# Attention emitted as products and sums, a new order of the first loads, and float64 weights converted in five instructions

## The chip, the cores and the metric

The kernel runs on one core of a Trainium2 chip. The metric is the device time of one execution, in microseconds (us). The core has five instruction streams that run beside each other, each strictly in its own order, and wait for each other on semaphores: TensorE (PE in the profile: matmuls; PEld: its weight loads), VectorE (DVE), ScalarE (ACT), GpSimd (POOL) and SyncE (SP, which here only issues DMAs). ACT issues a few DMAs too.

## The reference

For every token, a softmax over seven taps mixes the token's x with those of the six tokens before it, head by head; a layer with a "SoLU" activation and a layer norm follows.

```python
w = softmax(weight_gen)                       # B=8, S=4160, 8 heads, 7 taps
out[b, s, h, :] = sum_k w[b, s, h, k] * x_pad[b, s + k, h, :]      # D = 192 = 8 heads x 24
h = out.reshape(33280, 192) @ w_in            # 192 -> 1024
solu = h * softmax(h)
ln = (solu - mean) / sqrt(var + 1e-6) * g_ln
return ln @ w_out                             # 1024 -> 192
```

[...]

## The kernel before

**Tiling.** Partition p holds a run of 260 tokens in a row; tile t (0 to 259) is token t of all 128 runs. x and weight_gen come in chunks (4, 8, 8, then 15 of 16 tiles); buffers `xt` (two) and `wt` (three) take turns. Each run needs the six tokens before it, its halo; for chunk 0 the halo is loaded from the run before, and where a batch begins it has to be zero.

**Steps.** Each piece of work has a short name, a tile or chunk number and one engine:

- `t0` to `t6`, the softmax of the taps, once per chunk: `t0` DVE maximum (L112), `t1` POOL subtraction (L114), `t2` ACT exponential (L118), `t3` DVE sum (L120), `t4` ACT scale (L123), `t5` DVE reciprocal (L125), `t6` POOL multiplication (L127). `v00` to `v03` on ACT sum the squares of x (L148), in up to four parts that need the chunk's four x loads `lx0` to `lx3` (L90); `v1` to `v5` are tiny.
- `attA`, on POOL, once per group of 4 tiles (2 at the very start): the seven products tap by x (L180, into `pr`). `attB`, on POOL: their sums. In a two-part group (L190, L192) they leave two halves, which DVE adds (`fin`, L457); in a three-part group (L187, L188) three parts are left, and TensorE adds them as it transposes. Groups alternate, two parts first.
- `dup` on ACT (L463), `xT` on PE (transpose of two tiles, L477: 4 matmuls for a two-part group, 12 for a three-part one), `xhi` on ACT (L485), `xld` on DVE (L491).
- Per tile: `mm1` on PE (first layer, 12 matmuls, L503 and L506), `max` DVE (L518), `exp` ACT (L524), `solu` DVE (L532), `sq` ACT (L538), `hi` ACT (L545), `lo` DVE (L549), `tr` a transposing DMA from SP (L557), `mm2` on PE (second layer, 24 matmuls, L597), `out` on ACT (L608), which empties the one PSUM buffer `po` that the next `mm2` needs. `f0` to `f5` are small statistics.
- Once, at the start: the weights. `float_of_double` turns 512 (w_in) or 384 (w_out) doubles per partition into floats: three DVE operations, two ACT, three DVE (L250 to L269), for the parts `a0`, `b`, `a1` of w_in and `c0` to `c3` of w_out. `n0` to `n7` make one scale from w_in, `a03`, `a04`, `b3`, `b4` split it into two f16 halves; `q..` and `p..` do the like with w_out.

**Order.** `plan` lists all steps with an engine, a cost in ns, the steps that each must follow and a time before which it can't start. `issue_order` walks through that list as if the engines ran it, and picks on each free engine the ready step with the smallest tile number plus a constant per step name (`URGENCY`). The resulting list is emitted as it stands; the engines then keep this order, whatever the real times are. In `plan`, `attA` and `attB` are two steps. In the emitted program they are one: `attA` emits products and sums together, and `attB` emits nothing (`attB=lambda t: None`, L623). So where the list has another POOL step between the two, that step is emitted behind the sums.

**Start.** ahead of the list stand the loads, in the order of the code on SP and on ACT, the table load of ACT, the zeroing of the halo on POOL (L75), constants, and `t0` to `t3` of chunk 0. The halo of chunk 0 comes in eight DMAs of 15 partitions, four from each of SP and ACT (L79).

## Time and profile before

| what | value |
|---|---|
| time, median of 3 | 1321.08 us (1319.99 to 1323.04) |
| the profiled execution | 1321.71 us |
| its span, first to last instruction | 1319.7 us |
| mean granted TensorE clock | 0.991 |
| DVE busy | 1177.3 us (89%), 1816 instructions |
| ACT busy | 1182.3 us (90%), 2374 instructions |
| DMA | 210.38 MB, mean 159 GB/s |

The profile is of one execution; all its times count from the span's start. A row of the timeline has the start, the duration, engine, line, operation, and what is written and read; in brackets stands the idle time of the engine before it and what ended it. A row of the list of waits has who waited for whom, the sum in us, how often, and the longest. A row of the windows has for a stretch the busy time of each engine and, behind it, the granted TensorE clock. Four engines are within three points of each other, so a share of busy time alone does not say which one sets the time.

### The profile page before, as it was taken

How to read it: one execution, taken by the hardware profiler on the slowest of the kernel's cores; microseconds unless marked ns; L12 is line 12 of the kernel's file. 1: busy time of each engine (PE TensorE's matmuls, PEld its weight loads, DVE VectorE, ACT ScalarE, POOL GpSimd, SP SyncE). 2: the span in 40 equal slices, each digit the busy share in tenths (PEclk: the TensorE clock that was granted, in tenths of full speed). 3: DMA queues.
4: the chain of work that ended last, by engine and by line, in shares of the span. 5: the costliest groups of instructions: out<-in, count | busy, mean ns of one | idle time of the engine just before them, and what ended most of it. 6: DMA issues, size and time to landing. Idle time of an engine off the chain costs nothing.

```text
span 1319.7 us, 27156 instructions
## 1 busy us (share of the span) xinstructions
PE 1215.5 (92%) x10412; PEld 837.0 (63%) x10412; DVE 1177.3 (89%) x1816; ACT 1182.3 (90%) x2374; POOL 1190.1 (90%) x241
## 2 busy tenths in 40 slices
PE   0598989999999999999998999999999999999997
PEld 0255656666666666666665666666666666667766
DVE  5898889989999998989897898989989899999984
ACT  3799989988999999989897999989999999999885
POOL 4999899998999999999999999997999999999700
PEclk9999999999999999999999999999999999999999
DMA  6278669675867768595857759687775977777665
GB/s 183 75 184 188 125 146 187 142 200 137 189 144 188 174 155 173 138 217 122 209 138 155 162 144 191 135 199 141 173 179 137 196 144 189 149 135 126 145 144 116
DMA packets 565313, 210.38 MB, mean 159 GB/s; under 512 B 544456, under 2 KB 545864, under 8 KB 565184
## 3 DMA queue, kind: packets, MB, share of 16 engines
q1 hardware_dynamic: 563208, 206.55, 70.1%
q10 hardware_dynamic: 1976, 2.12, 0.6%
q8 instruction: 81, 1.33, 0.4%
q14 instruction: 48, 0.39, 0.1%
HBM read 46.15 MB, written 25.56 MB: 54 GB/s over the span
## 4 chain that ended last, share of the span: by engine, by line
POOL 27%; ACT 21%; PE 21%; DVE 14%; issue 12%; DMA 4%; SPq 1%; POOLq 0%; ACTq 0%; DVEq 0%
POOL pr L180 15%; PE po L597 8%; PE h L506 6%; ACT e L538 5%; ACT hl L545 5%; ACT e L524 5%; DVE hl L549 4%; POOL pr L190 4%; POOL wide L187 4%; PE h L503 3%; DVE h L518 3%; DVE h L532 3%; DMA xt<-in_x_dram 3%; POOL half L192 2%; PE pa L477 2%
## 5 line engine op out<-in xcount | busy, mean ns | idle before, releaser
L180 POOL TENSOR_TENSOR pr<-xt,wt 128x5376 f32<-128x5376 f32 (+1 forms) x66 | 631.0, 9561 | 3.1
L597 PE MATMUL po<-w_hl,hlT 128*128 128x192 f16 x6192 | 556.8, 247 | 37.3 <-ACT ot L608 34.8
L597 PEld LDWEIGHTS <-hlT 128*128 128x128 f16 x6240 | 525.8, 98 | 82.6 <-issue 46.4
L549 DVE SCALAR_TENSOR_TENSOR hl<-h,hl 128x1024 f16<-128x1024 f32 x260 | 315.5, 1220 | 71.8 <-ACT e L538 45.0
L532 DVE SCALAR_TENSOR_TENSOR h<-h,row,e 128x1024 f32<-128x1024 f32 x260 | 334.0, 1286 | 18.3 <-ACT e L524 15.4
L518 DVE TENSOR_SCALAR_CACHE_REDUCE h<-h,row 128x1024 f32<-128x1024 f32 x260 | 333.9, 1285 | 5.0 <-PE h L506 4.8
L524 ACT ACTIVATE e<-h,stats 128x1024 f32<-128x1024 f32 x260 | 293.5, 1129 | 8.2 <-DVE h L518 5.5
L545 ACT ACTIVATE hl<-h 128x1024 f16<-128x1024 f32 x260 | 267.1, 1028 | 32.7 <-DVE h L532 16.0
L538 ACT ACTIVATE e<-h,stats 128x1024 f32<-128x1024 f32 x260 | 292.5, 1125 | 2.7 <-DVE hl L549 2.5
L506 PE MATMUL h<-wa_hi,x_hi 128*128 128x512 f16 x520 | 200.9, 386 | 0.0
L506 PE MATMUL h<-wa_lo,x_hi 128*128 128x512 f16 x520 | 198.1, 381 | 0.0
L506 PE MATMUL h<-wa_hi,x_lo 128*128 128x512 f16 x520 | 198.1, 381 | 0.0
L506 PEld LDWEIGHTS <-x_hi 128*128 128x128 f16 x1040 | 80.6, 98 | 174.0 <-issue 113.1
L190 POOL TENSOR_TENSOR pr<-pr 128x2304 f32<-128x2304 f32 (+1 forms) x34 | 167.6, 4930 | 2.7
L187 POOL TENSOR_TENSOR wide<-pr 128x2304 f32<-128x2304 f32 x32 | 162.3, 5073 | 2.5
L608 ACT ACTIVATE ot<-po,stats 128x192 f32<-128x192 f32 x258 | 111.4, 432 | 6.8 <-PE po L597 6.8
L192 POOL TENSOR_TENSOR half<-pr 128x1536 f32<-128x1536 f32 (+1 forms) x34 | 113.9, 3349 | 2.7
L503 PE MATMUL h<-wb_hi,x_hi 64*128 64x512 f16 x520 | 102.3, 389 | 14.7 <-DVE hl L549 7.3
L503 PE MATMUL h<-wb_hi,x_lo 64*128 64x512 f16 x520 | 100.1, 380 | 0.0
L503 PE MATMUL h<-wb_lo,x_hi 64*128 64x512 f16 x520 | 100.1, 380 | 0.0
L477 PE MATMUL pa<-ident,wide 128*128 128x128 f32 x768 | 95.7, 275 | 3.9 <-ACT wide L463 3.9
L477 PEld LDWEIGHTS pa<-ident,wide 128*128 128x128 f32 x768 | 88.1, 142 | 13.3 <-ACT wide L463 4.0
(98 smaller groups left out, 1120.4 us busy)
## 6 DMA issues: line engine op xcount, KB each, us to landing
out_dram<-ot SPq DMA_DIRECT2D x65, 384.0 KB, 2.7
xt<-in_x_dram SPq DMA_DIRECT2D x30, 576.0 KB, 4.8
xt<-in_x_dram SPq DMA_DIRECT2D x30, 480.0 KB, 4.5
wt<-in_weight_gen_dram SPq DMA_DIRECT2D x15, 448.0 KB, 5.0
hlT<-hl SPq DMA_TRANSPOSE x260, 3.9
xt<-in_x_dram SPq DMA_DIRECT2D x3, 384.0 KB, 4.7
raw_a<-in_moe_w_in_dram ACTq DMA_DIRECT2D x2, 512.0 KB, 7.3
raw<-in_moe_w_out_dram ACTq DMA_DIRECT2D x1, 768.0 KB, 11.6
```

Of the source, the lines that this page charges most:

```text
L180: nc.gpsimd.tensor_tensor(out=window(pr, 0, [(TG * D, K), (HG, n * H), (1, HG)]), in0=window(xt, t * D, [(D, K), (HG, n * H), (1, HG)]), i ...
L187: nc.gpsimd.tensor_tensor(out=half, in0=pr[:, :3], in1=pr[:, 3:6], op=ALU.add)
L190: nc.gpsimd.tensor_tensor(out=pr[:, :3], in0=pr[:, :3], in1=pr[:, 3:6], op=ALU.add)
L503: nc.tensor.matmul(h[:, fs], lhs[rows, 1, :], rhs[rows], start=n == 0, stop=False)
L506: nc.tensor.matmul(h[:, fs], lhs[:, 0, :], rhs[:, fs], start=False, stop=n == 2)
L518: nc.vector.tensor_scalar(h, h, row(t, BACK), 3.0e38, op0=ALU.mult, op1=ALU.min, accum_out=stat(t, NMAX))
L524: nc.scalar.activation(e, h_of[t], AF.Exp, bias=stat(t, NMAX), scale=-1.0, accum_out=stat(t, Z))
L532: nc.vector.scalar_tensor_tensor(out=h, in0=h, scalar=row(t, SCALE), in1=e, op0=ALU.mult, op1=ALU.mult, accum_out=stat(t, M))
L538: nc.scalar.activation(e_of.pop(t), h_of[t], AF.Square, bias=stat(t, M), scale=-float(FF), accum_out=stat(t, Q),)
L545: nc.scalar.activation(hl[:, 0, :], h_of[t], AF.Copy, scale=2.0**14)
L549: nc.vector.scalar_tensor_tensor(out=hl[:, 1, :], in0=h_of[t], scalar=2.0**14, in1=hl[:, 0, :], op0=ALU.mult, op1=ALU.subtract,)
L597: nc.tensor.matmul(po[:, :D], hlT[:, half * NJ + j, :], w2_hl[:, j, w, :], start=n == 0, stop=n == len(terms) - 1,)
```

## The change

1. **Attention in two steps.** `attA` now emits the products alone (`products`), `attB` the sums (`add_up`, `sums`). The halves get two buffers, `a` three. Three-part groups now come first (33 of them, 32 two-part ones by sets of four tiles).
2. **First loads.** Chunk 0's halo comes in one DMA of 127 partitions on SP, across batch borders too; where a batch begins, DVE clears it with a bit mask (`x0`, `first_halo`), once `v00` has read it. ACT issues only the two halves of `raw_a` (w_in's first 128 rows); w_out, g and the rest go through SP, and chunk 1's load is put behind the first taps, its halo copy into the list (`x1`).
3. **Weights by bit fields.** A float's bits are taken from the two words of the double by shifts, masks and ORs: three DVE operations and, beside them, one ACT square of the high word read as a float; a fourth DVE operation multiplies by 0 where that square is too small. Every part has 512 numbers: six parts, where there were three of 512 and four of 384.
4. **Order.** `plan` has other costs, conditions and start times, `URGENCY` other numbers; so the whole list is another one.

The core of the diff:

```diff
-            nc.gpsimd.memset(xt[:, : HALO * D], 0.0)
             nc.sync.dma_start(xv[:, HALO : HALO + n, :], x_run[:, :n, :])
-            for b in range(B):
-                queue = nc.sync if b % 2 else nc.scalar
-                queue.dma_start(
-                    xv[b * PB + 1 : (b + 1) * PB, :HALO, :],
-                    x_run[b * PB : (b + 1) * PB - 1, RUN - HALO :, :],
-                )
+            nc.vector.memset(xt[:1, : HALO * D], 0.0)
+            nc.sync.dma_start(xv[1:, :HALO, :], x_run[: P - 1, RUN - HALO :, :])
...
-        if parts == 3:
-            nc.gpsimd.tensor_tensor(out=half, in0=pr[:, :3], in1=pr[:, 3:6], op=ALU.add)
-            nc.gpsimd.tensor_tensor(out=half[:, 2], in0=half[:, 2], in1=pr[:, 6], op=ALU.add)
+        return pr
+
+    def sums(pr, out, n):
+
+        if out.shape[1] == 3:
+            nc.gpsimd.tensor_tensor(out=out, in0=pr[:, :3], in1=pr[:, 3:6], op=ALU.add)
+            nc.gpsimd.tensor_tensor(out=out[:, 2], in0=out[:, 2], in1=pr[:, 6], op=ALU.add)
             return
...
+    def first_halo(step):
+        if step == 0:
+            before = xs[0][:, : HALO * D].bitcast(I32)
+            nc.vector.tensor_scalar(before, before, within, None, op0=ALU.bitwise_and)
+        else:
+            load_x(1, 1)
...
             nc.vector.tensor_scalar(
-                ex, high, 20, 0x7FF, op0=ALU.logical_shift_right, op1=ALU.bitwise_and
-            )
-            nc.vector.tensor_scalar(out.bitcast(I32), high, 0xFFFFF, None, op0=ALU.bitwise_and)
-
-            nc.vector.tensor_scalar(ex, ex, 896, 896 + 255, op0=ALU.max, op1=ALU.min)
+                bits, high, 3, 0x3FFFFFF8, op0=ALU.logical_shift_left, op1=ALU.bitwise_and
+            )
+            for scalar, word, op in ((-0x40000000, high, ALU.bitwise_and), (29, low, ALU.logical_shift_right)):
+                nc.vector.scalar_tensor_tensor(
+                    out=bits, in0=word, scalar=scalar, in1=bits, op0=op, op1=ALU.bitwise_or
+                )
         elif step == 1:
-            nc.scalar.activation(out, out.bitcast(I32), AF.Copy, bias=1.0, scale=2.0**-20)
-            nc.scalar.activation(ex, ex, AF.Copy, bias=-896.0 * 2**23, scale=2.0**23)
+            size = scratch[key, "size"] = big.tile([P, FH], F32, name="size")
+            nc.scalar.activation(size, high.bitcast(F32), AF.Square)
...
     def attend(t):
+        c = chunk_at(t)
+        pr_of[t] = products(xs[c], ws[c], t - starts[c], group(t))
+
+    def add_up(t):
         n = group(t)
...
+        sums(pr_of.pop(t), out, n)
...
-        attA=attend, attB=lambda t: None, fin=last_sum, dup=copy_columns, xT=transpose_x,
+        attA=attend, attB=add_up, fin=last_sum, dup=copy_columns, xT=transpose_x,
...
-    a00=248.1, a01=90.7, a02=-45.7, a03=55.5, a04=187.7, a10=-193.2, a11=-144.1, a12=167.9, a13=0.9,
+    a00=11.1, a01=-98.4, a02=25.1, a03=-179.2, a04=-48.9, a10=186.8, a11=18, a12=-184.5, a13=64.6,
...
-        add("mm1", t, PE, 2150, ("xld", t - t % 2), ("sq", t - 3), ("lo", t - 3), *after)
...
+        add("mm1", t, PE, 2065, ("xld", t - t % 2), *after)
```

How the program's order moves, at three places. The first is POOL around tile 144, in the middle of the run. Before, `t6` (L127), then products and sums of a two-part group, then `t1` (L114); in the list that `issue_order` makes, `t1` of chunk 164 stands between `attA 144` and `attB 144`:

```order
L127 TENSOR_TENSOR wt<-wt,wy 128x896
L180 TENSOR_TENSOR pr<-xt,wt 128x5376
L190 TENSOR_TENSOR pr<-pr 128x2304
L192 TENSOR_TENSOR half<-pr 128x1536
L114 TENSOR_TENSOR wt<-wt,wm 128x896
L180 TENSOR_TENSOR pr<-xt,wt 128x5376
L187 TENSOR_TENSOR wide<-pr 128x12x192
```

The same stretch of the changed program (`t6` is L122 now, products L178, `t1` L109, sums L192 with L194 or L189 with L190):

```order
L122 TENSOR_TENSOR wt<-wt,wy 128x896
L178 TENSOR_TENSOR pr<-xt,wt 128x5376
L109 TENSOR_TENSOR wt<-wt,wm 128x896
L192 TENSOR_TENSOR pr<-pr 128x2304
L194 TENSOR_TENSOR half<-pr 128x1536
L178 TENSOR_TENSOR pr<-xt,wt 128x5376
L189 TENSOR_TENSOR wide<-pr 128x12x192
L190 TENSOR_TENSOR wide<-wide,pr 128x4x192
```

`t1` now stands ahead of the sums of a group, and one group earlier than before: these are the products of tile 140, before they were those of 144. The next `t6` follows `t1` after three groups' products instead of two. The second place is DVE from its first tap operation. Before (L112, L120, L125 are `t0`, `t3`, `t5`; L154 is `v1`; L250 to L255 open the conversion of `raw_a`):

```order
L112 TENSOR_REDUCE wm<-wt 128x32
L120 TENSOR_REDUCE wm<-wt 128x32
L154 TENSOR_REDUCE row<-squares_x 128x1
L112 TENSOR_REDUCE wm<-wt 128x64
L250 TENSOR_SCALAR h<-raw_a 128x512
L253 TENSOR_SCALAR h<-raw_a 128x512
L255 TENSOR_SCALAR h<-h 128x512
L125 RECIPROCAL wy<-wy 128x32
```

After (L107, L115, L120 are `t0`, `t3`, `t5`; L149 is `v1`; L261 and L265 open the conversion, L274 ends it; L243 clears the halo):

```order
L107 TENSOR_REDUCE wm<-wt 128x32
L261 TENSOR_SCALAR h<-raw_a 128x512
L265 SCALAR_TENSOR_TENSOR h<-raw_a,h 128x512 x2
L149 TENSOR_REDUCE row<-squares_x 128x1
L224 TENSOR_SCALAR within<-within 128x1
L225 TENSOR_SCALAR within<-within 128x1
L243 TENSOR_SCALAR xt<-xt,within 128x1152
L115 TENSOR_REDUCE wm<-wt 128x32
L274 SCALAR_TENSOR_TENSOR h<-size,h 128x512
L120 RECIPROCAL wy<-wy 128x32
```

Chunk 1's `t0` (128x64) no longer stands ahead of chunk 0's reciprocal; the opening of the first conversion and the mask do. The third place is the start of PE. Before (L302 is `n4`, L477 the transposes of tiles 0 and 2, L357 sums over w_out, L503 opens `mm1` of tile 0):

```order
L302 MATMUL po<-sq,ones 128x3
L477 MATMUL pa<-ident,a 128x128 x4
L357 MATMUL po<-raw_a,ones 128x192 x4
L477 MATMUL pa<-ident,a 128x128 x4
L503 LDWEIGHTS x_hi
```

After (L309 is `n4`, L493 the transpose, L362 the sums over w_out, L519 opens `mm1`):

```order
L309 MATMUL po<-sq,ones 128x3
L493 MATMUL pa<-ident,wide 128x128 x12
L362 MATMUL po<-raw_a,ones 128x192 x4
L519 LDWEIGHTS x_hi
L519 MATMUL h<-wb_hi,x_hi 128x512
```

The first layer of tile 0 no longer stands behind the transpose of tiles 2 and 3.

More of the change, by code (lines that the diff above doesn't have):

```diff
@@ L172, in norm_x, with chunk_at, products @@
             nc.scalar.activation(row[:, EPS_Z], row[:, SCALE], AF.Copy, scale=-1e-12 * FF**1.5)
+    def chunk_at(t):
+        return max(n for n in range(NCHUNK) if starts[n] <= t)
     def row(t, which):
-        return row_of[max(n for n in range(NCHUNK) if starts[n] <= t)][:, which]
-    def attention(xt, wt, t, n, half, parts):
+        return row_of[chunk_at(t)][:, which]
+    def products(xt, wt, t, n):
         pr = att.tile([P, K, TG, D], F32, name="pr", bufs=1)[:, :, :n]
@@ L337, in convert @@
     def convert(f, step):
-        second[f] = float_of_double(
-            2 + f, raw_2[:, 2 * D * JP * f : 2 * D * JP * (f + 1)], JP * D, step
+        if step == 2 and "w2" not in second:
+            second["w2"] = att.tile([P, NJ, D], F32, name="raw_a", bufs=1)
+        out = second["w2"].rearrange("p j d -> p (j d)")[:, f * FH : (f + 1) * FH] if step == 2 else None
+        float_of_double(
+            ((1, 1), (2, 0), (2, 1))[f], raw_2[:, f * FF : (f + 1) * FF], step, out
         )
     def scale_and_sum(f, step):
-        if "w2" not in second:
-            second["w2"] = att.tile([P, NJ, D], F32, name="raw_a", bufs=1)
         w2 = second["w2"]
@@ L627, in tile_kernel @@
     )
+    for n in range(2):
+        ops[f"x{n}"] = once(first_halo, n)
     for n in range(5):
@@ L680, in plan @@
+    t2=44.1, t3=-111, t4=-150.2, t5=-33.5, t6=245.4, tr=13.9, v00=221, v01=162, v02=94.7, v03=234.3,
+    v1=-130.7, v2=160, v3=1, v4=87.6, v5=29.8, x0=-119.5, x1=-81.8, xT=-15.1, xhi=45.2, xld=182.9,
+)
+PARTS = ((3, True), (2, False))
+HALVES = 2
+def plan(run, starts, group, stat_group, loads, parts):
     PE, DVE, ACT, SP, POOL = range(5)
@@ L714, in plan @@
-    add("p30", 0, DVE, 868, ("q31", 0), ("mm1", 1))
-    once("p31", DVE, 868, "p30", "sq", "lo")
+    for n, part in enumerate(order):
+        at = weights[part]
+        once(part + "0", DVE, 2050, *([order[n - 1] + "0"] if n else []), ready=at)
+        after = [order[n - 1] + "1"] if n else []
+        once(part + "1", ACT, 620, *after, *([order[n - 2] + "2"] if n > 1 else []), ready=at)
+        after = [part + "0", part + "1"]
+        if part == "c0":
+            after += ["a11"]
+        elif n > 3:
+            after.append(order[n - 1] + "2")
+        once(part + "2", DVE, 700, *after)
+        if n < 3:
+            once(part + "3", ACT, 580, part + "2", "n7")
+            once(part + "4", DVE, 660, part + "3")
+            once(norm_of[part], DVE, 600, part + "2")
@@ L716, in plan @@
+    for f, part in enumerate(("c0", "c1", "c2", "c2")):
+        once(f"q{f}0", ACT, 770, part + "2", ready=16000)
+        once(f"q{f}1", PE, 660, f"q{f}0", *([f"q{f - 1}1"] if f else ["n5"]))
+        once(f"q{f}2", ACT, 520, f"q{f}0", "c22")
+    add("p30", 0, DVE, 880, ("q31", 0), ("mm1", 2), ("sq", 0), ("lo", 0))
+    add("p31", 0, DVE, 870, ("p30", 0), ("sq", 1), ("lo", 1))
     once("p5", PE, 220, "q02", "q12", "q22", "q32", "q31")
-    once("p6", DVE, 660, "p5")
+    once("p6", DVE, 1120, "p5")
@@ new lines, in plan @@
+        add("attA", t, POOL, 30 + 9690 * size, *after, ready=20000 if c == 1 else 0)
+        first = t // 4 * 4
+        after = [("attA", t)]
+        if summed:
+            k = wides.index(first)
+            after += reads(wides[k - 2]) if k > 1 else [("c20", 0), ("c21", 0)] if k == 1 else []
+        else:
+            k = halves.index(t)
+            after += [("fin", halves[k - HALVES])] if k >= HALVES else []
+        add("attB", t, POOL, (6865 if count == 3 else 8515) * size, *after)
@@ L800, in plan @@
+        if summed:
+            add("dup", t, ACT, (140 + 584 if count == 3 else 140 + 390) * size, ("attB", t))
+        else:
+            k = sums.index(first)
+            after = reads(sums[k - 3]) if k > 2 else []
+            add("fin", t, DVE, (2680 if count == 3 else 1700) * size, ("attB", t), *after)
+            add("dup", t, ACT, 90 + 250 * size, ("fin", t))
     for t in range(0, run, 2):
         g = group_of[t]
-        if three(t):
-            add("xT", t, PE, 1330, ("dup", g), ("xld", t - 2))
-        else:
-            add("xT", t, PE, 470, ("dup", g), ("xld", t - 2))
@@ L819, in plan @@
-        add("sq", t, ACT, 1094, ("solu", t))
-        add("hi", t, ACT, 913, ("solu", t), ("tr", t - 3))
-        add("lo", t, DVE, 1145, ("hi", t))
+        after = [("mm1", t - 1)]
+        if t < 6:
+            after += (
+                [("b4", 0), ("a04", 0), ("a14", 0), ("c10", 0)],
+                [("c02", 0)],
+                [("c12", 0), ("c22", 0)],
+                [("p31", 0), ("sq", 2), ("lo", 2)],
+                [("p80", 0)],
+                [("p81", 0)],
+            )[t]
+        else:
+            after += [("sq", t - 3), ("lo", t - 3)]
```

237 lines of the change are left out of this document (108 added, 129 removed).

## The prediction, made before the changed kernel ran

> **What bounds the kernel now.** I read the page's busy times first, then the list of waits, then timelines of POOL, PE and ACT, and windows at the places where PE stood still.
>
> ```profile
> PE 1215.5 (92%) x10412; PEld 837.0 (63%) x10412; DVE 1177.3 (89%) x1816; ACT 1182.3 (90%) x2374; POOL 1190.1 (90%) x241
> ...
> PE po L597 <- ACT ot L608: 34.8, 33, 6.4
> ...
> ACT wt L118 <- POOL wt L114: 26.2, 8, 7.5
> ...
> POOL wt L114 <- DVE wm L112: 22.3, 5, 13.4
> ACT junk L148 <- DMA xt<-in_x_dram: 21.9, 14, 3.3
> POOL wt L127 <- DVE wy L125: 20.8, 6, 7.0
> ```
>
> Four engines are almost equally loaded, so the loss is in waits that cross engines. One kind stands out: ACT, an engine without slack, waits 26.2 us for POOL's subtraction of the taps. First the pace without waits, of PE (transposes of successive pairs of tiles) and of POOL (products):
>
> ```profile
> 1233.27 0.60 PE L477 MATMUL pa<-ident,a 128*128 128x128 f32 x4
> ...
> 1241.97 0.60 PE L477 MATMUL pa<-ident,a 128*128 128x128 f32 x4
> ...
> 1250.68 1.47 PE L477 MATMUL pa<-ident,wide 128*128 128x128 f32 x12
> ...
> 1260.26 1.47 PE L477 MATMUL pa<-ident,wide 128*128 128x128 f32 x12
> ```
>
> A pair from a two-part group takes 1250.68 - 1241.97 = 8.71 us, one from a three-part group 1260.26 - 1250.68 = 9.58: on average 4.57 us per tile, 1189 us for 260 tiles.
>
> ```profile
> 1084.47 1.76 POOL L114 TENSOR_TENSOR wt<-wt,wm 128x896 f32<-128x896 f32 x1
> ...
> 1176.82 9.71 POOL L180 TENSOR_TENSOR pr<-xt,wt 128x5376 f32<-128x5376 f32 x1
> ...
> 1212.12 9.71 POOL L180 TENSOR_TENSOR pr<-xt,wt 128x5376 f32<-128x5376 f32 x1
> ...
> 1243.90 3.44 POOL L192 TENSOR_TENSOR half<-pr 128x1536 f32<-128x1536 f32 x1
> ```
>
> POOL needs 1212.12 - 1176.82 = 35.30 us for 8 tiles and two tap operations of 1.76 per 16: 4.63 us per tile. So POOL and PE run side by side, POOL a hair slower. POOL ends at 1247.3; PE and the rest need another 72.4 us. How far POOL is ahead, from the end of a group's sums to the first layer of its first tile, for tile 32 and tile 256:
>
> ```profile
> 192.18 3.45 POOL L192 TENSOR_TENSOR half<-pr 128x1536 f32<-128x1536 f32 x1
> ...
> 213.73 0.39 PE L503 MATMUL h<-wb_hi,x_hi 64*128 64x512 f16 x2 [0.31 <-DVE hl L549]
> ...
> 1281.46 0.39 PE L503 MATMUL h<-wb_hi,x_hi 64*128 64x512 f16 x2
> ```
>
> 18.1 us (195.6 to 213.7) at tile 32, 34 us (1247.3 to 1281.5) at the end: from tile 32 on PE is the slower one, by waits, not by work.
>
> Now the worst wait, on POOL, ACT and PE, and the windows over PE's clock behind three such waits (the number after the engines is the granted clock):
>
> ```profile
> 712.20 5.08 POOL L190 TENSOR_TENSOR pr<-pr 128x2304 f32<-128x2304 f32 x1
> ...
> 720.74 1.75 POOL L114 TENSOR_TENSOR wt<-wt,wm 128x896 f32<-128x896 f32 x1
> ...
> 722.52 0.95 ACT L118 ACTIVATE wt<-wt 128x896 f32<-128x896 f32 x1 [7.55 <-POOL wt L114]
> ...
> 726.61 3.49 PE L597 MATMUL po<-w_hl,hlT 128*128 128x192 f16 x24 [6.43 <-ACT ot L608]
> ```
> ```profile
> 179.90:183.30 3.40, 3.40 (x13) 1.22 (x10) 1.77 (x3) 3.40 (x7) 3.40 (x1) 0.50 0.00 0
> 275.40:278.80 3.40, 3.40 (x21) 1.88 (x18) 3.40 (x6) 3.17 (x5) 3.40 (x1) 0.51 1.12 285
> ...
> 722.60:729.40 6.80, 2.79 (x18) 2.65 (x18) 4.99 (x7) 6.79 (x11) 6.80 (x1) 0.50 0.42 94
> ```
>
> ACT has reached `t2`, whose `t1` stands on POOL behind 8.5 us of sums. Had `t1` been issued where the list puts it, ahead of the sums, it would have ended near 714, before ACT got there. While ACT waits, `out` does not empty `po`, PE stops, and its clock falls to half.
>
> **The change, part by part** (from the profiled execution: 1321.7 us, span 1319.7 and 2.0 around it; it is 0.6 above the median).
>
> *Two steps, middle of the run.* The seven chunks whose `t1` the old list put between a group's products and sums are 36, 52, 68, 84, 132, 164 and 196; ACT's waits for L114 after the start are seven, at exactly these. Chunks whose `t1` stood elsewhere have none. PE's stops behind them:
>
> ```profile
> 18.25 0.58 ACT L118 ACTIVATE wt<-wt 128x448 f32<-128x448 f32 x1 [5.21 <-POOL wt L114]
> ...
> 138.14 1.07 PE L597 MATMUL po<-w_hl,hlT 128*128 128x192 f16 x11 [1.31 <-ACT ot L608]
> ...
> 179.42 0.39 PE L503 MATMUL h<-wb_hi,x_hi 64*128 64x512 f16 x2 [2.81 <-ACT e L538]
> ...
> 274.43 0.74 PE L597 MATMUL po<-w_hl,hlT 128*128 128x192 f16 x7 [2.31 <-ACT ot L608]
> ...
> 330.24 0.39 PE L503 MATMUL h<-wb_hi,x_hi 64*128 64x512 f16 x2 [1.09 <-ACT e L538]
> ```
>
> 26.2 less the 5.21 of the start is 21.0 us on ACT. On PE: 1.31 + 2.81 + 2.31 + 1.09 + 6.43 = 13.95 us, and half of the busy time at half clock, (3.40 + 3.40 + 2.79) / 2 = 4.8. **Term: -18.8 us**; bounds 0 (ACT waits there for something else) and -21.0 - 4.8 = -25.8. On these rows the clock halves behind a stop of 2.31 us. The Trainium skill ("TensorE: Matmul & The Clock Gate", section "HAM oscillation — how this bites in real kernels") wants no idle gap longer than about 3.4 us; by that the gaps of 2.31 and 2.81 would have cost no clock and the sum would be 3.4 us higher. The rows decide.
>
> *POOL's own waits for `wy`.* `t6` waited 20.8 us in six places, because a late `t1` makes `t3` and `t5` late. Now `t1` is a group earlier and a whole group more lies between it and `t6`: I take 17 of the 20.8 away, leaving some for the start. POOL is ahead of PE (its last sums end 72.4 us before the end), so this is worth nothing alone, but it keeps POOL from becoming the bound: its end moves from 1247.3 to 1247.3 - 17 - 5.5 (below) = 1225.
>
> *The other waits of PE for `out`.* 34.8 - (1.31 + 2.31 + 6.43) = 24.7 us. Behind most in the middle stands ACT's wait for x (21.9 us, 14 times), whose loads SP issues in the list's order, between transposes that wait for `lo`. The old plan costed `mm1` at 2150 ns, while the pair's 8.71 us less the 0.60 of its transposes leaves 2.03 for each of its four products; so ACT arrived before its data. The new plan says 2065. Bounds 0 and -24.7; **I take -13**, near the middle, since the list is new but SP's pattern isn't.
>
> *First loads and conversion.* The path before:
>
> ```profile
> 1.20 0.42 SPq L76 DMA_DIRECT2D xt<-in_x_dram  x1
> ...
> 1.82 1.91 ACTq L79 DMA_DIRECT2D xt<-in_x_dram  x4
> ...
> 7.82 1.32 ACTq L216 DMA_DIRECT2D g<-in_moe_g_ln_dram  x1
> ...
> 9.49 1.79 ACT L148 ACTIVATE junk<-xt 128x1920 f32<-128x1920 f32 x1
> ...
> 16.54 0.62 DVE L112 TENSOR_REDUCE wm<-wt 128x64 f32<-128x448 f32 x1 [4.98 <-DMA wt<-in_weight_gen_dram]
> ...
> 18.53 0.70 DVE L255 TENSOR_SCALAR h<-h 128x512 int32<-128x512 int32 x1
> ...
> 19.14 0.34 DVE L125 RECIPROCAL wy<-wy 128x32 f32<-128x32 f32 x1
> ...
> 20.21 4.95 POOL L180 TENSOR_TENSOR pr<-xt,wt 128x2688 f32<-128x2688 f32 x1
> ...
> 48.57 0.61 PE L503 MATMUL h<-wb_hi,x_hi 64*128 64x512 f16 x2
> ```
> ```profile
> xt<-in_x_dram SPq DMA_DIRECT2D x3, 384.0 KB, 4.7
> raw_a<-in_moe_w_in_dram ACTq DMA_DIRECT2D x2, 512.0 KB, 7.3
> ```
>
> ACT issued DMAs from 1.82 until 9.14; the reciprocal stood on DVE behind chunk 1's maximum, which waited for its load, and a conversion. Now ACT is free early and its first DMA, at 1.82, is `raw_a`. With the 7.3 of the issue row `raw_a` lands near 9.1, its second half somewhat later; on DVE follow the conversion's opening (3 x 0.70), the mask (1152 numbers at 0.70 per 512: 1.6), and `v1`, `t3`, the closing operation and the reciprocal (an estimate of 1.6 from the rows' 0.34 and 0.70), on POOL `t6` (20.21 - 19.48 = 0.7): 15.1. If x alone decides (1.20 + 4.7 = 5.9, then 1.8 for L148 and the same without the opening), 11.6. I take 14.7, near the first: POOL starts **5.5 us earlier**; bounds -8.6 and 0. The conversion itself falls from 42 DVE operations to 24 of the 0.70 row, 9 us of DVE time beside POOL's work. Behind the reciprocal (14) stand some 30 DVE operations, most of 0.70, until the last split of w_in: 22 us, so PE's first layer starts near 37 instead of 48.6, no longer behind the transpose of tiles 2 and 3. But from tile 4 on PE gets its tiles from POOL: I cost those 11 us at nothing, and if POOL's products were late as before, they would stay worth nothing. The extra three-part group moves 1.6 us from POOL to 1.7 on PE: nothing. w_out and g move to SP's queue behind chunk 1's taps, and w_out lies in a `wide` buffer that tile 8's sums need: nothing, for it is read right after w_in's conversions, by 35, and those sums come near 65.
>
> A rule speaks against this part: the Trainium skill ("DMA: Bandwidth & Descriptors", section "Issuing engines are not separate DMA queues") says that transfers issued on several engines share the same 16 DMA engines and that only the issuing time is saved. By it the early `raw_a` would slow x, and the 5.5 us would be 0, the upper bound above.
>
> **Sum:** 1321.7 - 18.8 - 13 - 5.5 = **1284 us**. From POOL's side: 1225 + 72.4 - 16 (its lead of 34 us at the end back to the 18 of tile 32) + 2.0 = 1283. Both agree; what is late next is POOL's feed.
>
> **The rivals.** *All locks to POOL.* Every wait of ACT and `wm` goes too (22.3 us less the 13.4 of the start is 9): 1283 - 9 - a few = 1268 to 1274. For it: PE runs at its floor wherever no such wait lies near. Against: waits for x remain. *Only the start, or a wait of the new order in place of the old* (ACT meets `t1` late for another reason, such as `wm`): 1321.7 - 5.5 to 1321.7 - 5.5 - 18.8 = 1297 to 1316. For it: lists and real times drift apart. *Not what it says:* the split changes nothing, since ACT waits for x there instead, and the start is held by the loads: 1321. *Slower:* with `t1` between products and sums, a late DVE maximum holds up finished products, so each wait of POOL delays PE's feed too. Of the five `wm` waits one was 13.4, at the start, the others average 2.2. POOL has 22.5 + 16 us to lose; with 14 chunks it is lost from a mean wait of 2.8 us per chunk on; at the longest `wy` wait, 7.0 per chunk, 14 x 7.0 - 38.5 makes 1381, at 4.0 per chunk 1339. Against it: outside the start `wm` was late only four times in 1300 us.
>
> **How the numbers follow.** The forecast (1276 to 1296) 0.58; locked to POOL (1264 to 1276) 0.20; start only or new waits (1296 to 1318) 0.13; no change 0.03; slower 0.06. The range 1264 to 1302 leaves out about 2 in 10. Within 0.2% (2.6 us, about what a measurement here can tell from no change): 0.03; faster 0.91; slower 0.06.
>
> **What would show it.** In the new profile ACT's wait for POOL's subtraction should be under 5 us in all after the start, with no half clock in the middle; POOL's wait for `wy` under 5; POOL's first product near 14.7, its last sums near 1225, PE's first layer near 37. I am wrong if ACT waits at `t2` as long as before, if POOL stands between products and sums, or if the waits for x grow.

## The result, and the profile after

The changed kernel takes **1333.99 us** (median of 4 runs, 1328.66 to 1334.77); the kernel before took 1321.24 beside it. The medians differ by 12.8 us, and the ratio is 1.0087 (95% interval 1.0058 to 1.0116): slower by about 1%, where 1284 us and a range of 1264 to 1302 had been forecast. The profiled execution is the quickest of the four (1328.66 us, span 1326.9, mean clock 0.993; the other three have 0.987 to 0.990), so its trace shows some 5 us less than the median.

Busy times and waits of the changed kernel (who waited for whom, us in total, times, longest):

```profile
PE 1212.0 (91%) x10428; PEld 835.8 (63%) x10428; DVE 1166.0 (88%) x1800; ACT 1179.7 (89%) x2366; POOL 1187.2 (89%) x241
...
ACT junk L143 <- DMA xt<-in_x_dram: 69.2, 29, 31.3
...
PE po L613 <- ACT ot L624: 33.9, 21, 3.0
POOL wt L122 <- DMA xt<-in_x_dram: 32.2, 1, 32.2
...
POOL wt L122 <- DVE wy L120: 28.5, 12, 3.7
...
POOL wt L109 <- DVE wm L107: 6.8, 2, 4.3
...
ACT wt L113 <- POOL wt L109: 2.1, 1, 2.1
```

The last line is the one that the change was predicted to move: ACT's waits for POOL's subtraction were 26.2 us and are 2.1. The work is hardly changed. But two other lines have grown: ACT's waits for x, 21.9 us before, are 69.2, of which 31.3 in one piece, and POOL's waits for `wy`, 20.8 before, are 28.5, now 12 times, about once in a chunk.

**The start.** Rows of the timeline of the changed kernel, of SP's queue, ACT, POOL and PE (start, duration, line; idle time before in brackets):

```profile
1.65 0.32 SPq L75 DMA_DIRECT2D xt<-in_x_dram  x1
2.02 12.99 SPq L208 DMA_DIRECT2D hl<-in_moe_w_in_dram  x1
...
33.31 1.80 ACT L143 ACTIVATE junk<-xt 128x1920 f32<-128x1920 f32 x1 [31.30 <-DMA xt<-in_x_dram]
...
38.40 0.57 POOL L122 TENSOR_TENSOR wt<-wt,wy 128x224 f32<-128x224 f32 x1 [32.17 <-DMA xt<-in_x_dram]
39.05 4.95 POOL L178 TENSOR_TENSOR pr<-xt,wt 128x2688 f32<-128x2688 f32 x1
...
57.94 0.61 PE L519 MATMUL h<-wb_hi,x_hi 64*128 64x512 f16 x2
```

L75 is the new transfer of the 127 boundary rows. It is issued at 1.65, and the squares over x, which need it, wait until 33.31; POOL's first product starts at 39.05 instead of 20.21, 18.8 us later. PE's first layer comes at 57.94 (48.57 before). The windows of the same kernel (after the engines: granted clock, DMA share, GB/s) show what the DMA does meanwhile:

```profile
8.00:12.00 4.00, 0.00 (x0) 0.00 (x0) 0.00 (x0) 0.00 (x0) 0.00 (x0) 1.00 0.06 25
12.00:16.00 4.00, 0.00 (x0) 0.00 (x0) 0.00 (x0) 0.00 (x0) 0.00 (x0) 1.00 0.07 28
```

All engines stand still, and the 16 DMA engines are 0.06 to 0.07 busy: one of 16 is 0.0625. The 127 packets of 4608 bytes, one for each boundary row, run from 6.8 to 32.7 us in the trace; from 16 us on other loads run beside them.

**The end.** POOL's last sums (row below) end at 1268.2, against 1247.3 before and 1225 forecast.

```profile
1266.40 1.82 POOL L190 TENSOR_TENSOR wide<-wide,pr 128x768 f32<-128x768 f32 x1
```

So POOL is 18.8 us late at its first product and 20.9 at its last. From there to the end of the span it takes 1326.9 - 1268.2 = 58.7 us instead of 72.4: PE stays closer behind POOL, as was forecast, but POOL does not run faster.

**The middle.** Chunk 212 of the changed kernel, SP's queue first:

```profile
967.30 0.42 SPq L85 DMA_DIRECT2D xt<-in_x_dram  x1
970.47 4.43 SPq L573 DMA_TRANSPOSE hlT<-hl  x2
974.95 0.97 SPq L85 DMA_DIRECT2D xt<-in_x_dram  x1
976.27 3.52 SPq L573 DMA_TRANSPOSE hlT<-hl  x1
979.84 0.57 SPq L85 DMA_DIRECT2D xt<-in_x_dram  x1
980.51 3.74 SPq L573 DMA_TRANSPOSE hlT<-hl  x1
...
984.91 0.42 SPq L85 DMA_DIRECT2D xt<-in_x_dram  x1
```

and what waits for it on ACT and POOL:

```profile
989.64 0.84 ACT L143 ACTIVATE junk<-xt 128x768 f32<-128x768 f32 x1 [1.60 <-DMA xt<-in_x_dram]
...
1005.67 0.48 ACT L118 ACTIVATE wy<-wm,row 128x128 f32<-128x128 f32 x1
...
1007.97 1.76 POOL L122 TENSOR_TENSOR wt<-wt,wy 128x896 f32<-128x896 f32 x1 [2.16 <-DVE wy L120]
...
1046.58 9.70 POOL L178 TENSOR_TENSOR pr<-xt,wt 128x5376 f32<-128x5376 f32 x1
```

The four parts of x are issued over 17.6 us (967.30 to 984.91), because SP takes its queue in order and the transposes between them hold it for 3.5 to 4.4 us at a time. ACT, which must square the parts in its own order, waits; the norm that follows from the squares comes late to `wy`; and POOL waits 2.16 us at `t6` (L122), though that chunk's first product (1046.58) is still 38 us away. Which of these three waits costs the time can't be read off: the experiments below take them away one at a time.

### The profile page after: what moved, and what is told of

Same layout as the page of the kernel before. It is cut to its first block, busy times and chain, and to the rows that moved or that the text cites. A ratio compares the mean times of both kernels' runs of the same rounds, so it can differ in the third digit from the quotient of the medians.

```text
span 1326.9 us, 27167 instructions
## 1 busy us (share of the span) xinstructions
PE 1212.0 (91%) x10428; PEld 835.8 (63%) x10428; DVE 1166.0 (88%) x1800; ACT 1179.7 (89%) x2366; POOL 1187.2 (89%) x241
## 4 chain that ended last, share of the span: by engine, by line
PE 57%; ACT 15%; DMA 11%; issue 5%; DVE 5%; POOL 4%; SPq 1%; ACTq 0%; DVEq 0%; POOLq 0%
PE po L613 25%; PE h L522 18%; DMA xt<-in_x_dram 11%; PE h L519 10%; PE pa L493 5%; ACT e L540 4%; ACT hl L561 4%; ACT e L554 4%; DVE hl L565 2%; POOL pr L178 2%; SPq L573 1%; DVE h L534 1%; ACT ot L624 1%; DVE h L548 1%; ACT x_hi L501 1%
## 5 line engine op out<-in xcount | busy, mean ns | idle before, releaser
L178 POOL TENSOR_TENSOR pr<-xt,wt 128x5376 f32<-128x5376 f32 (+1 forms) x66 | 630.9, 9558 | 3.9
L534 DVE TENSOR_SCALAR_CACHE_REDUCE h<-h,row 128x1024 f32<-128x1024 f32 x260 | 334.4, 1286 | 11.9 <-PE h L522 10.4
L189 POOL TENSOR_TENSOR wide<-pr 128x2304 f32<-128x2304 f32 (+1 forms) x34 | 167.6, 4929 | 2.3
L192 POOL TENSOR_TENSOR pr<-pr 128x2304 f32<-128x2304 f32 x32 | 162.3, 5072 | 1.5
L143 ACT ACTIVATE junk<-xt 128x768 f32<-128x768 f32 (+2 forms) x63 | 56.5, 897 | 69.2 <-DMA xt<-in_x_dram 69.2
L519 PE MATMUL h<-wb_hi,x_hi 64*128 64x512 f16 x520 | 102.0, 388 | 15.5 <-ACT e L554 12.6
L194 POOL TENSOR_TENSOR half<-pr 128x1536 f32<-128x1536 f32 x32 | 110.4, 3449 | 2.5
L493 PE MATMUL pa<-ident,wide 128*128 128x128 f32 x792 | 99.1, 275 | 1.6 <-DVE x_lo L507 1.1
L519 PE MATMUL h<-wb_lo,x_hi 64*128 64x512 f16 x520 | 99.7, 379 | 0.0
L519 PE MATMUL h<-wb_hi,x_lo 64*128 64x512 f16 x520 | 99.6, 378 | 0.1
```

The source lines that it names most:

```text
L178: nc.gpsimd.tensor_tensor(out=window(pr, 0, [(TG * D, K), (HG, n * H), (1, HG)]), in0=window(xt, t * D, [(D, K), (HG, n * H), (1, HG)]), i ...
L189: nc.gpsimd.tensor_tensor(out=out, in0=pr[:, :3], in1=pr[:, 3:6], op=ALU.add)
L493: nc.tensor.matmul(pa[:, n, i, :], source, ident, is_transpose=True, start=at == 0, stop=at == len(terms) - 1,)
L519: nc.tensor.matmul(h[:, fs], lhs[rows, 1, :], rhs[rows], start=n == 0, stop=False)
L534: nc.vector.tensor_scalar(h, h, row(t, BACK), 3.0e38, op0=ALU.mult, op1=ALU.min, accum_out=stat(t, NMAX))
```

## The experiments

Two theories stood at the outset. **A**: the transfer of 127 partitions runs over one DMA engine and delays the start; the rest of the loss is a wait in each chunk. **B**: the start is late because w_in is now loaded by ACT's queue at the same time, or because the new order is slower by itself. All times are medians of 4 to 10 runs; a ratio is to the kernel before, run beside it and can differ a little from that of the medians. PE's gaps are those over 0.9 us between 270 and 1100 us, added up from the timeline.

| run | us | ratio (95%) | ACT waits for x, us | PE's gaps, us |
|---|---|---|---|---|
| before | 1321.2 | | 21.9 | 19.1 |
| changed | 1334.0 | 1.0087 (1.0058 to 1.0116) | 69.2 | 18.4 |
| changed, halo 112 + 15 | 1312.0 | 0.9935 (0.9911 to 0.9960) | 51.4 | 21.6 |
| changed, halo 126 + 1 | 1312.6 | 0.9940 (0.9921 to 0.9959) | 48.8 | 19.9 |
| before, halo 127 | 1342.7 | 1.0167 (1.0146 to 1.0188) | 54.2 | 20.5 |
| before, cut in two | 1310.4 | 0.9918 (0.9893 to 0.9944) | 29.0 | 18.7 |
| halo 112 + 15, not cut | 1366.6 | 1.0327 (1.0301 to 1.0353) | 51.2 | 45.0 |
| halo 112 + 15, t6 later | 1314.6 | 0.9937 (0.9921 to 0.9953) | 52.2 | 21.5 |
| halo 112 + 15, squares later | 1299.7 | 0.9828 (0.9808 to 0.9849) | 9.1 | 0 |
| **halo 112 + 15, loads together** | **1279.2** | 0.9680 (0.9658 to 0.9703) | 9.2 | 0 |
| changed, loads together | 1300.5 | 0.9856 (0.9828 to 0.9884) | 31.9 | 0 |
| before, cut, loads together | 1294.9 | 0.9803 (0.9781 to 0.9824) | 1.5 | 6.0 |
| before, loads together | 1312.7 | 0.9941 (0.9919 to 0.9962) | 1.5 | 16.3 |

### The boundary rows in two transfers

```diff
-            nc.sync.dma_start(xv[1:, :HALO, :], x_run[: P - 1, RUN - HALO :, :])
+            for p0, p1 in ((1, 113), (113, P)):
+                nc.sync.dma_start(xv[p0:p1, :HALO, :], x_run[p0 - 1 : p1 - 1, RUN - HALO :, :])
```

> The changed kernel with the 127 boundary rows of chunk 0 loaded as two transfers, of 112 and of 15 partitions; nothing else differs. Theory A (one transfer of 127 partitions moves through 1 of 16 DMA engines, at the 25-28 GB/s that the windows show for 8 to 32 us, and all loads of the start wait behind it): the boundary rows land before 15 us, DVE's sums of squares of chunk 0 are done before 20 us, POOL's first product starts between 14 and 21 us instead of 39.0, and since POOL is the pace from there on, the time falls by as much: 1310 to 1316 us. Rival B (the start is late because w_in is now fetched on ACT's queue and takes bandwidth from x, or because of the order of the other loads): POOL's first product stays later than 33 us and the time within 5 us of 1334. In both, the one wait of POOL for wy in each chunk of 16 tiles (28.5 us in 12 waits) stays.

Measured: 1311.95 us, 22.0 less than the changed kernel and now faster than before. A window and POOL's first product of this kernel:

```profile
8.00:12.00 4.00, 0.00 (x0) 0.00 (x0) 0.00 (x0) 1.17 (x1) 0.00 (x0) 1.00 1.03 239
```
```profile
16.58 4.94 POOL L179 TENSOR_TENSOR pr<-xt,wt 128x2688 f32<-128x2688 f32 x1
```

The same bytes, w_in on the same queue, and the DMA engines are full instead of at one sixteenth; the 127 rows' packets now run from 6.0 to 9.9 us, and POOL starts 22.5 us earlier. Theory B of the start falls. (The windows of the changed kernel show 25 to 28 GB/s from 8 to 16 us, not until 32 as the expectation says; from 16 to 32 us they show 89 to 201 GB/s, with the other loads.) POOL's waits for `wy` did not stay at 28.5 us but grew to 45.2, in 14 waits.

### The same with 126 partitions and 1

```diff
+            for p0, p1 in ((1, P - 1), (P - 1, P)):
```

> The changed kernel with the same boundary rows as one transfer of 126 partitions and one of 1: almost the size of the slow transfer, with a count of partitions that 14 divides. Theory A (the count 127, a prime, is what puts the transfer on one engine): the windows from 2 to 10 us show over 200 GB/s and none the 25-28 GB/s of one engine, POOL's first product within 3 us of that of the run with 112 and 15 partitions, and the time within 4 us of it. Rival C (one large transfer with 4.5 KB in each partition is slow by its size or its pattern, or because eight transfers became one): the boundary rows land after 28 us and the time is within 5 us of 1334.

Measured: 1312.6 us, 0.7 from the run above; POOL's first product at 18.0.

```profile
8.00:12.00 4.00, 0.00 (x0) 0.00 (x0) 0.48 (x3) 0.00 (x0) 0.00 (x0) 1.00 1.02 216
18.01 4.94 POOL L179 TENSOR_TENSOR pr<-xt,wt 128x2688 f32<-128x2688 f32 x1
```

(The first line is of its windows, the second of its timeline.) A transfer one row smaller has no trouble: it is the count 127, not size, pattern or the merging of eight transfers. The Trainium skill ("DMA: Bandwidth & Descriptors", section "🔬 Why a DMA increments its semaphore by 16 and not by 1") says how a count sets this: a transfer is spread over the largest number of engines, up to 16, that divides the outermost size of both its sides, and 127 partitions, a prime, get one. The traces agree: a share of 0.06 and 25 GB/s at 127; 1.02 and 216 GB/s at 126, with the other loads beside it.

### The kernel before with the one transfer

```diff
-            for b in range(B):
-                queue = nc.sync if b % 2 else nc.scalar
...
+            nc.sync.dma_start(xv[1:, :HALO, :], x_run[: P - 1, RUN - HALO :, :])
```

> The kernel before with its eight transfers of boundary rows for chunk 0 replaced by the one transfer of 127 partitions on SP's queue. The rows in front of the seven later sequences are loaded rather than set to zero, so those tiles take their taps from the sequence before and the zeroing is left out. Theory A: the start alone makes the loss, so POOL's first product moves from 20.2 to 33-39 us and the time grows by 13 to 19 us, to 1334-1340. Rival B (the transfer is harmless and the loss comes from the rest of the change): the first product within 3 us of 20.2 and the time within 4 us of 1321.

Measured: 1342.73 us, 22.0 more than before (this kernel leaves out the zeroing where a batch begins, so its output differs there); POOL's first product moves from 20.21 to 39.86. The loss is 3 us above what was expected, and it goes from the start to the end undiminished: +22 in the old order, -22 in the new.

### The cut alone, in the old order

```diff
-        attention(xs[c], ws[c], t - starts[c], n, half, parts)
+        pr_of[t] = products(xs[c], ws[c], t - starts[c], n)
...
-        attB=lambda t: None,
+        attB=add_up,
```

> The kernel before with only the attention step cut in two: its products are emitted where they stood, its sums at the place that the planner already gave them, so that a chunk's subtraction t1 stands between the two on POOL. Loads, conversion and order are those of before. Theory of the prediction's first term: ACT's waits for POOL's subtraction fall from 26.2 us to under 5, the stretches at half clock in the middle of the run go, and the time falls by 14 to 19 us, to 1302-1307. Rival D (POOL, not PE, is the pace behind those waits, so that only what its own waits give back is gained): the ACT waits go, but the time falls by no more than 5 us. Rival E (the cut shifts POOL's other work, the taps and t6, into a wait of its own): POOL's waits for wy grow above 20.8 us and the time is the same or longer.

Measured: 1310.35 us, 10.3 less than before, under the 14 to 19 expected. Its waits:

```profile
ACT junk L148 <- DMA xt<-in_x_dram: 29.0, 15, 4.7
...
POOL wt L127 <- DVE wy L125: 9.5, 5, 5.7
...
ACT wt L118 <- POOL wt L114: 4.1, 1, 4.1
```

The wait for the subtraction has gone (26.2 to 4.1), POOL's for `wy` has halved, and yet PE's gaps are 18.7 us where they were 19.1. One of them, ACT ahead of PE:

```profile
345.79 0.84 ACT L148 ACTIVATE junk<-xt 128x768 f32<-128x768 f32 x1 [2.96 <-DMA xt<-in_x_dram]
...
351.29 0.96 PE L607 MATMUL po<-w_hl,hlT 128*128 128x192 f16 x5 [3.44 <-ACT ot L618]
```

ACT no longer stands at `t2`; it reaches the squares sooner and stands there, for x, and PE behind it as before. In the old order the next late thing was x.

### The cut undone, in the new order

```diff
+        add_up(t)
...
-        attB=add_up,
+        attB=lambda t: None,
```

> The changed kernel with the boundary rows in two transfers of 112 and 15 partitions (1311.95 us), and with the sums of a group put right behind its products again, everything else in the new order: the cut of the attention step undone. Theory (the cut is worth its waits also in the new order): ACT's waits for POOL's subtraction t1 rise from 2.1 us to over 15 and the time to 1317-1327. Rival (the new order puts t1 so that the cut brings nothing): the waits stay under 6 us and the time within 3 us of 1312.

Measured: 1366.63 us, 54.7 more than with the cut, where 5 to 15 had been expected.

```profile
POOL wt L123 <- DVE wy L121: 94.2, 14, 10.0
...
PE po L615 <- ACT ot L626: 68.2, 37, 3.6
...
ACT wt L114 <- POOL wt L110: 54.5, 14, 5.8
```

The new order puts `t1` between products and sums in nearly every chunk (14 waits), so without the cut each chunk pays, on ACT at `t2` and on POOL at `t6`. The cut is necessary for this order; in the old one it mends seven places.

### POOL's wait in each chunk

```diff
+        if op == "t6" and t >= 36:
+            held.append((op, t))
+            continue
+        order.append((op, t))
+        if op == "attB":
+            order += held
+            held = []
```

> The changed kernel with the boundary rows in two transfers of 112 and 15 partitions (1311.95 us), and with each chunk's last product of its taps (t6, from tile 36 on) issued behind the sums of the next group instead of at the moment that the planner calls it ready; nothing else moves. Theory G (POOL is the pace and loses 1.7 to 3.7 us a chunk, waiting for wy at a t6 that stands one group too early): POOL's waits for wy fall from 45.2 us to 15 or less, its last sums come 20 to 30 us earlier, and the time is 1287 to 1297. Rival H (POOL's wait is only the visible end of late x: PE's stop in each chunk, behind ACT's wait for x, stays and PE becomes the bound): the waits for wy go, PE's gaps of 1.6 to 2.7 us in each chunk stay, and the time falls by less than 6 us, to 1306-1312.

Measured: 1314.56 us: nothing gained, 2.6 us above the upper end of what rival H expects. The waits:

```profile
ACT junk L144 <- DMA xt<-in_x_dram: 52.2, 28, 9.3
...
PE po L614 <- ACT ot L625: 38.5, 21, 3.8
...
POOL wt L110 <- DVE wm L108: 35.9, 13, 4.2
...
POOL wt L123 <- DVE wy L121: 10.4, 1, 10.4
```

POOL's wait for `wy` is gone (45.2 to 10.4, the rest at the start), and 29 us of wait for `wm`, two steps of the next chunk further on, stand in its place; PE's gaps stay at 21.5 us. POOL's wait was the visible end of something else, and taking it away moved it. POOL's last sums end 5.7 us earlier than in the run that only repairs the start (1247.0 for 1252.7), but from there to the end PE needs 64.8 us instead of 58.7. That speaks for rival H: x is late, and PE's stop behind it counts.

### Moving the squares, or moving the loads

Two ways to take ACT out of its wait for x. Later squares (with all that follows from them, `t6` later still):

```diff
+    late = dict.fromkeys(("v00", "v01", "v02", "v03", "v1", "v2", "v3", "v4", "v5", "t4", "t5"), 24)
+    late["t6"] = 48
+    place = [(i + (late.get(op, 0) if t >= 36 else 0), i) for i, (op, t) in enumerate(order)]
```

> As the run with t6 later, by another way that also takes ACT out of its wait for x: from tile 36 on a chunk's squares of x and the steps that follow from them are issued 24 steps of the whole program's order later, t6 48 steps later; the loads of x stay. Theory G+H (both waits cost): ACT's waits for x fall from 51.4 us to under 20, PE has no gap over 1.3 us in the middle, and the time is 1283 to 1294, below the run with t6 alone by 4 us or more. If only POOL's wait counts: within 4 us of that run. If the later squares collide with other work of ACT: above it.

Earlier loads, with ACT's work where it was:

```diff
+        if op in ("lx1", "lx2", "lx3") and t >= 36:
+            continue
         ops[op](t)
+        if op == "lx0" and t >= 36:
+            for n in range(1, LOADS):
+                ops[f"lx{n}"](t)
```

> The changed kernel with the boundary rows in two transfers of 112 and 15 partitions (1311.95 us), and with the four loads of a chunk's x (from tile 36 on) issued one behind the other on SP's queue, where the new order has transposes of hl between them. ACT's work and t6 stay where they are. Theory J (x comes late because SP stands at each transpose for 4 to 5 us, waiting for hl, before it issues the next part of x): ACT's waits for x fall from 51.4 us to under 20, POOL's for wy from 45.2 to under 20, PE's gaps of 1.6 to 2.7 us in each chunk go, and the time is 1296 to 1304, like that of the run with the squares later (1299.68). Rival K (x is late because its buffer comes free late or its transfer is slow): the waits for x stay above 35 us and the time within 4 us of 1312. Rival L (the transposes behind the four loads are then late): PE waits for hlT, and the time is over 1306.

Measured: 1299.68 us with the squares later, 12.3 under the run that only repairs the start, where 18 to 29 had been expected; **1279.15 us** with the loads together, 32.8 under it and beyond every expectation. SP's queue in the second kernel, one chunk, and its waits:

```profile
921.44 2.05 SPq L86 DMA_DIRECT2D xt<-in_x_dram  x4
924.56 13.24 SPq L574 DMA_TRANSPOSE hlT<-hl  x4
```
```profile
POOL wt L123 <- DVE wy L121: 10.4, 2, 10.2
ACT junk L144 <- DMA xt<-in_x_dram: 9.2, 1, 9.2
...
PE po L614 <- ACT ot L625: 8.7, 9, 2.2
```

Four parts in 2.05 us instead of 17.6, and all three kinds of wait are gone outside the start: ACT's for x, POOL's for `wy` (two waits, 10.2 of them at the start) and PE's gaps. Theory J's cause holds, though its time (1296 to 1304) was 17 us too long; K and L fall. The transposes behind the loads do come a little late (ACT waits 12.3 us in all for `hlT`'s DMA), which costs PE no gap. From POOL's last sums to the end 58.7 us pass in the run that only repairs the start (span 1311.4) and 58.4 here (span 1273.6): in both, the time follows POOL's end, and that came 37.5 us earlier (1215.2 for 1252.7), near the 34.8 us by which POOL's waits for `wy` fell.

With the squares later, x is no longer waited for either, but POOL still stands:

```profile
POOL wt L110 <- DVE wm L108: 21.4, 11, 4.5
```

POOL's last sums end at 1234.9, 19.7 us after those of the kernel with the loads together, which is most of the 24.6 us between the two profiled executions. PE pays in small change as well: `PE h <- ACT e` has 16 waits instead of 5 and `PE pa <- ACT a` 14 instead of 10. Three runs more went this way, and none brought what its theory expected. The same for the kernel before with the cut:

> The kernel before with the attention step cut in two (1310.35 us), and with the squares of x and what follows from them issued 24 steps later, t6 48 steps later. There the gain of the cut was 10.3 us where 18.8 were predicted, PE's gaps between 270 and 1100 us hardly shrank (19.1 to 18.7 us), and ACT's waits for x rose from 21.9 to 29.0 us. Theory (ACT, no longer held by POOL, stands at the next load of x instead, and PE waits behind it as before): the waits for x fall under 10 us, PE's gaps over 0.9 us between 270 and 1100 us fall under 7 us, and the time is 1292 to 1301. Rival (those gaps of PE are of another cause, PE's pace is what it is): the waits for x go and the time stays within 4 us of 1310.

Measured 1312.75 us (ratio 0.9922, 0.9907 to 0.9938), no gain on 1310.35, as its rival had it; the waits for x went (1.7 us are left), and PE's gaps fell to 13.4 us only, 8.1 of them now in front of its first layer, waiting for DVE. That x was nonetheless the cause there, the old order with the loads together shows below. With `t1` to `t3` later too:

> The run with a chunk's squares and what follows 24 steps later and t6 48 steps later (1299.68 us), with t1, t2 and t3 of the chunk also 24 steps later. There POOL still waited 21.4 us in 11 waits for wm ahead of t1. If POOL's waits set the pace: they fall under 8 us and the time to 1289-1296. If PE's own pace and its small waits for ACT do: the waits go and the time stays within 3 us of 1299.7.

Measured 1310.6 us (0.9921, 0.9903 to 0.9940): POOL's waits for `wm` went (4.1 us are left), waits for `wy` (30.1 us) came; neither expectation was met. With the loads together as well:

> The run with a chunk's squares and what follows 24 steps later and t6 48 steps later (1299.68 us), with the four loads of x also issued together. Theory J and rival K alike expect no more waits for x to be taken away (9.1 us are left, all at the start): within 3 us of 1299.7. More than 4 us longer would be the price of loads that stand ahead of transposes; more than 4 us shorter a gain of SP's queue that the theories don't know.

Measured 1319.1 us (0.9993, 0.9965 to 1.0020; ten runs from 1309.3 to 1327.1), 19 us more than without: here POOL waits 32.7 us for `wm`, and PE for ACT's `a` in each chunk. So loads together are no gain in every order. Why these three are as slow as they are stays open; in each a shift of a chunk's steps by a fixed count took one wait away and another came, where the earlier load alone took the cause away.

### Do the two losses add, and what does the cut bring without late x?

The changed kernel with the loads together, halo as it is:

> The changed kernel with the four loads of a chunk's x issued together, and the boundary rows still in one transfer of 127 partitions. If the late start and the late x are two losses that add: 1334 less the 32.8 us that the loads together brought with the start repaired, 1297 to 1305, faster than before. If a later start hides part of it (POOL further behind PE, so that x has more time): over 1308.

Measured: 1300.54 us, 33.5 less than the changed kernel (32.8 with the start repaired). They add.

The kernel before, cut, with the loads together, and the kernel before with the loads together alone:

> The kernel before with the attention step cut in two (1310.35 us) and the four loads of a chunk's x issued together; order, start and conversion are those of before. Theory J (the cut's missing 8.5 us were taken by ACT's waits for x, 29.0 us, behind which PE stops): the waits for x fall under 8 us, PE's gaps over 0.9 us between 270 and 1100 us from 18.7 to under 6 us, and the time is 1285 to 1298. Rival (the old order has other waits ready, as it had when the squares were moved later): the gaps come back in front of other lines and the time is 1305 to 1313.

> The kernel before with nothing but the four loads of a chunk's x issued together. Theory J: ACT's waits for x fall from 21.9 to under 6 us and the time by 5 to 14 us, to 1307-1316, while ACT's waits for POOL's subtraction (26.2 us) stay or grow. Rival (with ACT held by POOL, earlier x is worth nothing): within 4 us of 1321.

Measured: 1294.9 and 1312.7 us, both within what theory J said (PE's gaps with the cut, at 6.0 us, only just). ACT's and PE's waits with the cut, then without it (where those for x are 1.5 us too):

```profile
PE po L607 <- ACT ot L618: 15.9, 24, 2.3
...
ACT wt L118 <- POOL wt L114: 6.5, 3, 4.8
...
ACT junk L148 <- DMA xt<-in_x_dram: 1.5, 1, 1.5
```
```profile
ACT wt L118 <- POOL wt L114: 28.0, 8, 9.9
PE po L597 <- ACT ot L608: 27.1, 28, 8.7
```

With early x, the cut is worth 1312.7 - 1294.9 = 17.8 us; with late x it was worth 10.3. Each alone gives 10.3 and 8.9 us against the kernel before beside it, both together 26.7: behind either wait stands the other.

## Why the prediction was wrong, point by point

**The start (term -5.5, bounds -8.6 and 0): failed, and with it the range.** It came out as +18.8 us at POOL's first product. The step that failed is the landing of x, "If x alone decides (1.20 + 4.7 = 5.9 ...)": the 4.7 us are the row of loads such as chunk 0's x, of 128 partitions, and the new transfer of 127, which the squares need as well, has no time in the sum at all. In the changed kernel x was there at 33.3, not 5.9. The change was described with that transfer, but neither its price nor the chance that it is slower than the eight that it replaces was weighed; "bounds -8.6 and 0" therefore left a loss out altogether. With the count mended, POOL starts at 16.6 (14.7 forecast, so -3.6 for -5.5) and PE's first layer at 35.5 (37 forecast). That is near, but by luck in part: the step let `raw_a` decide, and there it is x that decides. DVE reads `raw_a` from 5.55 on, and ACT waits for x until 10.83, 4.9 us after the 5.9. How much of that lateness comes of the sharing of the DMA engines that the prediction weighed (they are full in the window above) no run separates; in the changed kernel sharing did not decide, since from 8 to 16 us only about one engine worked.

**The other waits for `out` (term -13): failed, with the wrong sign for its cause.** The prediction saw that SP issues the loads of x between transposes, and then argued that new costs in the plan (2065 for 2150 at `mm1`) would let ACT come at the right time. The middle's waits for x rose from 21.9 to 69.2 - 31.3 = 37.9 us, and PE's gaps stayed (19.1, then 18.4). What sets them is SP's queue: loads together take 33 us off, two and a half times the term. The prediction had named growing waits for x as a sign that it is wrong, and it came. This step would have been enough: with only the start mended the time is 1312.0, still outside the range, and with only the loads together it is 1300.5, inside.

**The cut (term -18.8): mechanism right; alone it brings less.** ACT's waits for POOL's subtraction went from 26.2 to 2.1 us as forecast, and one half-clock stretch of 3.4 us was left in the middle of the profiled run. In the old order alone it is worth 10.3, since ACT then waits for x; once x is early it is worth 17.8, near the term. So the terms of the cut and of x were not independent, and adding them hid that the first needs the second. In the new order the cut is worth 54.7 us, which no step of the prediction had: the new order counts on it at nearly every chunk.

**"I take 17 of the 20.8 away" at POOL's `wy`: failed.** The waits became 28.5 us plus 32.2 for the first x. The prediction supposed a group more of room between `t1` and `t6`; what makes `wy` late is not `t1` but the norm, that is, x. POOL's end, forecast at 1225, was 1268.2: of these 43.2 us 24.3 come of the start (39.05 for 14.7), and the other 18.9 arose between the first product and the last sums, where a wait in each chunk stayed. In the kernel with both repairs it is 1215.2.

**The conversion:** four DVE operations of 0.67 to 0.70 us, as costed, and a square on ACT of 0.64 to 0.67. On DVE they are off the path to the first product (with the count mended, the reciprocal behind them waits 0.90 us for ACT); on ACT two squares, 1.21 us together, stand there between the squares of x and the norm. The mask took 0.82 us where 1.6 was estimated.

**The rivals.** The one that ended slower (POOL held by a late `wm` between products and sums) is not what happened: those waits fell to 6.8 us. "A wait of the new order in place of the old" came true in the middle, but its 1297 to 1316 holds only with the start repaired (1312.0). That the two things together would be slower than before was in no rival. "All locks to POOL" is what the kernel with both repairs shows: POOL's waits after the start are all but gone there, at 1279.2 us where that rival gave 1268 to 1274.

**What is left.** Both repairs give 1279.2 us, 54.8 less than the changed kernel and 41.4 less than the kernel before beside it. Against the old order with the cut and the early loads (1294.9) that is 15.7 us, which the new order, the start and the conversion share. Between the two profiled executions, 18.9 us apart, 6.1 us lie ahead of POOL's last sums and 12.8 behind them (71.2 us against 58.4); which part of the change brings them stays open. What was forecast for the whole change is near what it brings without these two faults; that does not mend the forecast, which rested on reading them as harmless.

## What to carry to other kernels

When a change merges or reshapes transfers, price the new one by its own count of partitions and not by its neighbours' bytes; a start in which the DMA share is 0.06, one engine of 16, points at its cause. A queue that a DMA shares with instructions that wait is part of that DMA's latency: put a tile's loads one behind the other ahead of the waiting ones, before moving the work that needs them (worth 9 to 33 us in four kernels here, though it cost 19 us in a fifth, whose steps had been shifted). And where several waits follow from one another, take away the earliest: here one of POOL's that was taken away came back two steps later, and two waits in series hid each other's gain.

## What the runs showed of the hardware

One DMA engine moved 25 to 28 GB/s of rows of 4.5 KB, and later transfers on the same queue stood behind it: SP needed 12.99 us to issue the next one (row L208 above, against 1.21 us for two of them with the transfer split).

How long PE stands still doesn't alone decide whether its clock halves. In the changed kernel a gap of 2.20 us was followed by half clock and one of 2.88 us was not:

```profile
231.82 0.90 PE L613 MATMUL po<-w_hl,hlT 128*128 128x192 f16 x9 [2.88 <-ACT ot L624]
...
385.99 1.31 PE L613 MATMUL po<-w_hl,hlT 128*128 128x192 f16 x12 [2.20 <-ACT ot L624]
```

How the gap lies counts too. In all 16 traces half clock begins only at times that are a whole number of steps of 3.413 us apart (in the changed kernel at 72.82 and 386.85, 92 steps). On that grid the gap of 2.20 us lies whole in one step, and that of 2.88 is cut at 229.83 into 0.89 and 1.99. The windows of these steps and of those behind them (PE's busy time is the first after the length, the clock the third number from the right):

```profile
229.83:233.25 3.42, 1.43 (x18) 1.43 (x18) 3.34 (x5) 3.42 (x9) 3.34 (x2) 1.00 0.27 52
233.25:236.66 3.41, 3.02 (x22) 1.33 (x19) 3.41 (x4) 3.41 (x7) 3.41 (x1) 1.00 0.54 102
383.43:386.85 3.42, 1.22 (x13) 0.94 (x12) 2.77 (x3) 3.42 (x7) 3.42 (x1) 1.00 0.14 30
386.85:390.26 3.41, 3.41 (x22) 2.18 (x19) 3.41 (x6) 3.41 (x8) 3.34 (x1) 0.50 0.73 139
```

Counted over the 16 traces, from 100 us to 60 us before the end: each of the 36 steps at full clock in which PE stood for more than 2.01 us was followed by half clock, none of the 5289 with less than 1.76 us was, and between the two it was 12 of 35. So what a gap costs here depends on where it falls on that grid; whether this also makes the 6 us by which the changed kernel's runs spread (clocks 0.987 to 0.993) is not shown.
